# A rolled loop for TensorE's sums, a small first tile and a short second pass in a channel-attention kernel

## The chip, the cores and the metric

The kernel runs on one core of a Trainium2 chip. The time of a run is the device time in microseconds of one launch. Besides, one execution was recorded by the hardware profiler; its span goes from the program's first instruction to its last.

A core has five engines that run side by side, each with its own queue of instructions: TensorE (PE in the profile), VectorE (DVE), ScalarE (ACT), GpSimd (POOL) and SyncE (SP). Sixteen DMA engines move data between the chip's memory and the core's own memory, SBUF. SyncE and ScalarE each own a DMA queue (q1 and q10 in the profile), and a DMA that is issued on either is split evenly over the 16 DMA engines. TensorE writes its results into another memory, PSUM.

## The reference

The input `x` has 384 x 384 pixels of 384 channels in bfloat16, 113 MB, and the output has the same size. Each channel is averaged over all pixels, multiplied by one weight, put through a sigmoid, and the whole channel is multiplied by the result:

```python
g = jnp.einsum("bhwc->bc", x) / (H * W)
...
for i in range(k):
    s = s + gp[:, i:i + C] * w1d[i]
s = _sigmoid(s)
return x * s[:, None, None, :]
```

Here `k` is 1, so there is one weight and no neighbouring channel. The numbers in `x` are normal with a deviation of 0.05, so that every channel's average is almost zero and every scale is close to sigmoid(0) = 0.5.

## The kernel before, in words

A scale depends on all pixels, so a plain kernel would read `x` twice. This one reads it once: it works out an early scale from the first tile of pixels, multiplies every tile by it and stores the result, and meanwhile sums all of `x`. At the end it works out the true scale and compares it, in bfloat16, with the early one. Only where the two differ in any channel does a second pass read `x` again and store the right product. In this data they are the same, and the second pass is skipped by a branch.

**Tiles.** The pixels are cut into 1152 "rows" of 128 x 384 numbers, one pixel for each of SBUF's 128 partitions; a row takes 768 B of each partition. The arena holds 272 rows and is used as six slots of 44 rows. There are 27 tiles (`sizes`, line 165): 25 of 44 rows, one of 28 and one of 24. Tile `k` lies in slot `k % 6`. In `dram` (line 129) each partition gets pixels that are next to each other, so a tile of 44 rows is 128 pieces of 33792 B, eight for each DMA engine.

**Loads.** The first four tiles (`BOTH`, line 115) are loaded in halves, one on SyncE's queue and one on ScalarE's, in packets of 16896 B; the weight follows the first half on ScalarE's queue (line 281). All later tiles are loaded on SyncE's queue alone. From the seventh tile on a load must wait until the store of the tile six back has landed (`Planner.dma`, line 80, works out the waits).

**Sums.** `add_rows` (line 199) multiplies a tile by a matrix of ones, 33 matmuls of 128 x 512 for 44 rows, and lets them add up in three PSUM banks: group 0 for the first tile (its sum gives the early scale), group 1 for all others. The first matmul is line 185, the others are line 187. All 864 are written out one after another in TensorE's program.

**Early scale.** VectorE adds the banks' six parts (`add_banks`, lines 227 and 229), ScalarE takes the sigmoid (line 288).

**Gate and store.** `put` (line 234) multiplies a tile by the early scale on VectorE (line 159), in place, so after TensorE has summed the tile; the store goes out on ScalarE's queue. The last tile alone is written to another slot (line 306), so that its gate needs only its load.

**Order.** `Planner` keeps a stream of operations for each engine and works out which semaphores each must wait for. The streams are emitted in the order in which the Python code adds them: in the loop of line 297, for tile `k`, the gate and store of tile `k - 6`, the load of `k`, the sum of `k`. The first loads go out ahead of everything else (`heads`, line 282).

**End.** After the last tile VectorE adds group 1 to the total, ScalarE takes the sigmoid (line 312), VectorE compares (320), reduces (328) and converts to a flag (334). In `second_pass` (line 362) SyncE, VectorE and ScalarE each load the flag and branch past the second pass, 27 tiles of load, gate and store in their programs. ScalarE then waits for all stores (line 398).

Of the kernel before, what the change touches and what calls it, by code (L numbers as in the profile page):

```python
# [3 lines left out]
P = 128  # L4
ROW = 384
BF16 = mybir.dt.bfloat16
# [7 lines left out]
class Planner:  # L14
# [9 lines left out]
    def __init__(self, nc, name, n_dma_sems):  # L24
        self.nc = nc
        self.streams = {e: [] for e in ("sync", "scalar", "vector", "tensor", "gpsimd")}
        self.sems = {e: nc.alloc_semaphore(f"{name}_{e}") for e in self.COMPUTE}
        self.count = {e: 0 for e in self.COMPUTE}
        self.pool = [nc.alloc_semaphore(f"{name}_dma_{i}") for i in range(n_dma_sems)]
        self.pool_uses = [0] * n_dma_sems  # L30
        self.n_dma = 0
        self.writer = {}
        self.readers = {}
        self.seen = {e: {} for e in self.streams}
        self.final = []

    def _wait(self, engine, token):
        sem, value = token
        if self.seen[engine].get(sem.name, 0) >= value:
            return  # L40
        self.seen[engine][sem.name] = value
        self.streams[engine].append(("wait", sem, value))

    def _needs(self, reads, writes):
        need = {}
        tokens = []
        for r in reads:
            if r in self.writer:
                tokens.append(self.writer[r])
        for r in writes:  # L50
            if r in self.writer:
                tokens.append(self.writer[r])
            tokens.extend(self.readers.get(r, ()))
        for sem, value in tokens:
            if need.get(sem.name, (None, 0))[1] < value:
                need[sem.name] = (sem, value)
        return list(need.values())

    def _record(self, token, reads, writes):
        for r in reads:  # L60
# [5 lines left out]
    def op(self, engine, emit, reads=(), writes=(), signal=True):  # L66


        reads, writes = list(reads), list(writes)
        for token in self._needs(reads, writes):  # L70
            if engine == "tensor" and token[0].name == self.sems["tensor"].name:
                continue
            self._wait(engine, token)
        token = (self.sems[engine], self.count[engine] + 1)
        if signal:
            self.count[engine] += 1
        self.streams[engine].append(("op", emit, self.sems[engine] if signal else None, 1))
        self._record(token, reads, writes)

    def dma(self, engine, out, in_, reads=(), writes=()):  # L80
        reads, writes = list(reads), list(writes)
        for token in self._needs(reads, writes):
            self._wait(engine, token)
        i = self.n_dma % len(self.pool)
        self.n_dma += 1
        if self.pool_uses[i]:
            self._wait(engine, (self.pool[i], 16 * self.pool_uses[i]))
        self.pool_uses[i] += 1
        token = (self.pool[i], 16 * self.pool_uses[i])
        self.streams[engine].append(  # L90
            ("op", lambda e: e.dma_start(out, in_), self.pool[i], 16)  # L91
        )
        self._record(token, reads, writes)
        return token

    def emit(self, name, e, most=None):

        now = self.streams[name][:most]
        del self.streams[name][: len(now)]
        for kind, a, b, *c in now:  # L100
            if kind == "wait":
                e.wait_ge(a, b)
            else:
                ins = a(e)
                if b is not None:
                    ins.then_inc(b, c[0])
# [5 lines left out]


WIDE = 512
EDGE, SLOT, BOTH = 44, 44, 4


def bass_standalone__channel_attn_eca__vision_kernel(
# [12 lines left out]

    ones = nc.alloc_sbuf_tensor("ones", [P, P], BF16)
    s_early = nc.alloc_sbuf_tensor("s_early", [P, C], BF16)
    s_true = nc.alloc_sbuf_tensor("s_true", [P, C], BF16)
    w_one = nc.alloc_sbuf_tensor("w_one", [1, 16], BF16)
    w_scaled = nc.alloc_sbuf_tensor("w_scaled", [P, 2], F32)
    warm = nc.alloc_sbuf_tensor("warm", [P, 2], F32)
    wrong = nc.alloc_sbuf_tensor("wrong", [P, 1], F32)
    redo = nc.alloc_sbuf_tensor("redo", [P, 1], I32)
# [18 lines left out]
        v, to_v = (at(r, n).rearrange("p (t c) -> p t c", t=n) for r in (place, to))  # L158
        return lambda e: e.tensor_tensor(to_v, v, s_b, ALU.mult)  # L159

    n_slots = n_arena // SLOT
    full, rest = divmod(n_rows - EDGE, SLOT)
    if rest < EDGE:
        full, rest = full - 1, rest + SLOT
    sizes = [EDGE] + [SLOT] * full + [4 * q for q in split(rest // 4, EDGE // 4)]
    assert sum(sizes) == n_rows and max(sizes) <= SLOT
    plan = Planner(nc, "a", 50)

    def load(place, n, r0, queues=("sync",)):
        of = dram(x_rows, r0, n)  # L170
        i = 0
        for queue, m in zip(queues, split(n, -(-n // len(queues)))):
            plan.dma(
                queue,
                at(place + i, m),
                of[:, i * C : (i + m) * C],
                writes=rows(place + i, m),
            )
            i += m
# [16 lines left out]
            )  # L196
        )

    def add_rows(place, n, group, first, last):

        n_wide = n * C // WIDE
        start = place * C
        for i in range(n_wide):
            bank = acc[group][i % 3]
            plan.op(
                "tensor",
                lambda e, i=i, bank=bank: mm(e,
                    bank[:, :],
                    ones[:],
                    arena[:, start + i * WIDE : start + (i + 1) * WIDE],  # L210
                    start=first and i < 3,
                    stop=last and i >= n_wide - 3,
                ),
                reads=["ones"] + (rows(place, n) if i in (0, n_wide - 1) else []),
                writes=[f"acc{group}"],
                signal=i == n_wide - 1,
            )

    def add_banks(group, copy):

# [10 lines left out]
                )  # L231
            plan.op("vector", emit, reads=[f"acc{group}", "total"], writes=["total"])

    def put(place, n, r0, to):
        plan.op(
            "vector",
            gate(to, place, n, s_early),
            reads=["s_early"] + rows(place, n),
            writes=rows(to, n),
        )  # L240
        plan.final.append(
            plan.dma("scalar", dram(o_rows, r0, n), at(to, n), reads=rows(to, n))
        )

    def weight():
# [12 lines left out]
            reads=["ones", "w_one"],  # L258
            writes=["w_all"],
        )  # L260
        for i, n in enumerate((sizes[0], n_rows)):
            plan.op(
                "vector",
                lambda e, i=i, n=n: e.tensor_scalar_mul(  # L264
# [3 lines left out]
                writes=[f"w_scaled{i}"],  # L268
            )

    starts = [sum(sizes[:k]) for k in range(len(sizes))]
    places = [k % n_slots * SLOT for k in range(len(sizes))]
    last = len(sizes) - 1


    plan.op("gpsimd", lambda e: e.memset(warm[:, 0:1], 0.0), writes=["warm"])  # L276
    plan.op("vector", lambda e: e.memset(ones[:], 1.0), writes=["ones"])  # L277
    for k in range(BOTH):
        load(places[k], sizes[k], starts[k], ("sync", "scalar"))
        if k == 0:  # L280
            plan.dma("scalar", w_one[0:1, 0:1], w1d.unsqueeze(0), writes=["w_one"])
    heads = {e: len(plan.streams[e]) for e in ("sync", "scalar")}
    weight()
    add_rows(places[0], sizes[0], 0, True, True)
    add_banks(0, copy=True)
    plan.op(
        "scalar",
# [3 lines left out]
        reads=["total", "w_scaled0", "warm1"],  # L291
        writes=["s_early"],
    )

    for k in range(1, len(sizes)):
        if k >= n_slots:
            j = k - n_slots
            put(places[j], sizes[j], starts[j], places[j])  # L300
        if k >= BOTH:
            load(places[k], sizes[k], starts[k])
        add_rows(places[k], sizes[k], 1, k == 1, k == last)
    for k in range(len(sizes) - n_slots, last):
        put(places[k], sizes[k], starts[k], places[k])
    put(places[last], sizes[last], starts[last], places[last + 1 - n_slots])


    add_banks(1, copy=False)
    plan.op(  # L310
        "scalar",
        lambda e: e.activation(  # L312
            s_true[:], total[:], ACT_F.Sigmoid, scale=w_scaled[:, 1:2]
        ),
        reads=["total", "w_scaled1"],
        writes=["s_true"],
    )
    plan.op(
        "vector",
        lambda e: e.tensor_tensor(  # L320
            total[:], s_true[:].bitcast(U16), s_early[:].bitcast(U16), ALU.not_equal
        ),
        reads=["s_true", "s_early"],
        writes=["total"],
# [13 lines left out]
    checked = (plan.sems["vector"], plan.count["vector"])  # L338


    again = Planner(nc, "b", 50)
    for place, n, r0 in zip(places, sizes, starts):
        again.dma("sync", at(place, n), dram(x_rows, r0, n), writes=rows(place, n))
        again.op(
            "vector",
            gate(place, place, n, s_true),
            reads=rows(place, n),
            writes=rows(place, n),
        )
        again.final.append(  # L350
            again.dma("scalar", dram(o_rows, r0, n), at(place, n), reads=rows(place, n))
        )
    for token in again.final:
        again._wait("scalar", token)
    stored = nc.alloc_semaphore("stored")
# [71 lines left out]
```

## Time and profile before

| what | us |
|---|---|
| median of 8 runs | 529.92 (529.63 to 530.01) |
| the profiled execution | 530.15 |
| its span, first to last instruction | 528.69 |
| TensorE busy, of that | 242.5 |
| VectorE busy | 241.2 |
| ScalarE busy | 2.7 |
| last load has landed, last gate starts | 496.45 |
| last store is issued | 501.4 |
| flag of the second pass is ready | 507.2 |

| DMA | |
|---|---|
| bytes moved | 226.57 MB |
| mean rate over the span | 429 GB/s |
| a load on SyncE's queue, 44 rows, issue to landing | 38.4 us |
| a store, 44 rows, issue to landing | 62.4 us |

The page lists busy time by engine, then the span in 40 slices, then the DMA queues with their packets, megabytes and share of the 16 engines' time. The queues q8 and q14, called "instruction", carry the engines' own programs from the chip's memory. In a line of the timeline the columns are start, length, engine, line, operation, and in brackets how long the engine sat idle before it and what ended that. A busy TensorE is not TensorE at its peak, and idle time of an engine that is not the bottleneck costs nothing. The trace also holds each DMA packet's start, length, queue and size.

### The profile page before, as it was taken

The page shows a single profiled execution, that of the slowest core. Times are in us where ns is not written, and L with a number is a line of the kernel's source. Part 1 is how long each engine was busy: PE and PEld are TensorE (multiplying, and loading weights), DVE is VectorE, ACT ScalarE, POOL GpSimd, SP SyncE. Part 2 cuts the span into 40 slices and gives each one's busy share as a digit, 9 for nine tenths or more (in the row PEclk, how much of TensorE's full clock was granted, in tenths as well). Part 3 has the DMA queues.
Part 4 walks back from the last instruction along what each step waited for, and adds up shares of the span by engine and source line. Part 5 has one row for each costly group of instructions (what it writes and reads, how often), then busy time and mean ns, then how long its engine had stood idle before and what let it go on. Part 6 is the DMA issues. An engine that isn't in the chain of part 4 may idle for free.

```text
span 528.7 us, 1091 instructions
## 1 busy us (share of the span) xinstructions
PE 242.5 (46%) x865; PEld 0.2 (0%) x2; DVE 241.2 (46%) x45; ACT 2.7 (1%) x4; POOL 0.3 (0%) x5
## 2 busy tenths in 40 slices
PE   0876356065165274274164274374363363375400
PEld 0000000000000000000000000000000000000000
DVE  0199741632633624624624624615624615616720
ACT  1000000000000000000000000000000000000000
POOL 0000000000000000000000000000000000000000
PEclk9998786686786786776786886775786876876765
DMA  8999999999999999999999999999999999999998
GB/s 358 431 426 422 447 412 446 435 427 442 417 447 424 437 442 417 447 421 440 435 424 445 422 442 435 424 445 417 445 433 424 442 419 445 426 444 419 446 421 351
DMA packets 8360, 226.57 MB, mean 429 GB/s; under 512 B 930, under 2 KB 930, under 8 KB 930
## 3 DMA queue, kind: packets, MB, share of 16 engines
q10 hardware_dynamic: 4466, 121.90, 53.5%
q1 hardware_dynamic: 3888, 104.60, 46.1%
q8 instruction: 3, 0.05, 0.0%
q14 instruction: 3, 0.02, 0.0%
HBM read 113.25 MB, written 113.25 MB: 428 GB/s over the span
## 4 chain that ended last, share of the span: by engine, by line
another core or an unknown queue 70%; DMA 16%; DVE 4%; PE 3%; SPq 1%; issue 1%; ACT 0%; ACTq 0%
DMA out_dram<-arena 8%; DMA arena<-in_x_dram 6%; PE acc L187 3%; DVE arena L159 3%; DMA w_one<-in_w1d_dram 2%; SPq L91 1%; DVE total L229 1%; ACT s_early L288 0%; ACT s_true L312 0%; DVE total L227 0%; DVE total L320 0%; DVE wrong L328 0%; PE acc L185 0%; ACTq L91 0%
## 5 line engine op out<-in xcount | busy, mean ns | idle before, releaser
L187 PE MATMUL acc<-arena,ones 128*128 128x512 bf16 x863 | 242.0, 450 | 245.7 <-DMA arena<-in_x_dram 245.7
L159 DVE TENSOR_TENSOR arena<-arena,s_early 128x16896 bf16<-128x16896 bf16 (+2 forms) x27 | 234.5, 8692 | 240.2 <-PE acc L187 237.4
L255 PE MATMUL w_all<-w_one,ones 1*128 1x1 bf16 x1 | 0.2, 158 | 14.3 <-DMA w_one<-in_w1d_dram 14.3
L264 DVE TENSOR_SCALAR w_scaled<-w_all 128x1 f32<-128x1 f32 x2 | 0.2, 154 | 13.5 <-PE w_all L255 13.5
L229 DVE TENSOR_TENSOR total<-total,acc 128x128 f32<-128x128 f32 (+2 forms) x11 | 4.5, 409 | 1.4 <-PE acc L187 1.1
L227 DVE COPY total<-acc 128x384 f32<-128x384 f32 x1 | 0.6, 558 | 9.3 <-PE acc L187 9.3
L312 ACT ACTIVATE s_true<-total,w_scaled 128x384 bf16<-128x384 f32 x1 | 0.6, 616 | 477.8 <-DVE total L229 477.8
L249 ACT ACT_TABLE_LOAD x1 | 1.3, 1283 | 3.4 <-issue 3.4
L320 DVE TENSOR_TENSOR total<-s_true,s_early 128x384 f32<-128x384 uint16 x1 | 0.6, 558 | 0.7 <-ACT s_true L312 0.7
L288 ACT ACTIVATE s_early<-total,w_scaled 128x384 bf16<-128x384 f32 x1 | 0.6, 617 | 21.9 <-DVE total L229 21.9
L185 PE MATMUL acc<-arena,ones 128*128 128x512 bf16 x1 | 0.6, 586 | 0.0
L328 DVE TENSOR_REDUCE wrong<-total 128x1 f32<-128x384 f32 x1 | 0.6, 553 | 0.0
L277 DVE MEMSET ones<- 128x128 bf16 x1 | 0.2, 165 | 0.8 <-PEq L412 0.8
L249 ACT ACTIVATE warm<-warm 128x1 f32<-128x1 f32 x1 | 0.2, 203 | 0.0
L334 DVE CAST redo<-wrong 128x1 int32<-128x1 f32 x1 | 0.2, 153 | 0.0
L255 PEld LDWEIGHTS w_all<-w_one,ones 1*128 1x128 bf16 x1 | 0.1, 101 | 14.2 <-issue 14.2
L185 PEld LDWEIGHTS acc<-arena,ones 128*128 128x128 bf16 x1 | 0.1, 102 | 0.0
L412 POOL MEMSET const-bfloat16-1.0<- 128x1 bf16 x1 | 0.1, 102 | 0.0
L412 POOL MEMSET const-uint8-127<- 128x1 uint8 x1 | 0.1, 102 | 0.0
L276 POOL MEMSET warm<- 128x1 f32 x1 | 0.1, 99 | 0.3 <-POOLq L412 0.3
L412 POOL MEMSET const-float32-0.0<- 128x1 f32 x1 | 0.1, 99 | 0.2 <-issue 0.2
L412 POOL MEMSET const-float32-1.0<- 128x1 f32 x1 | 0.1, 99 | 0.0
## 6 DMA issues: line engine op xcount, KB each, us to landing
out_dram<-arena ACTq DMA_DIRECT2D x25, 4224.0 KB, 62.4
arena<-in_x_dram SPq DMA_DIRECT2D x21, 4224.0 KB, 38.4
arena<-in_x_dram ACTq DMA_DIRECT2D x4, 2112.0 KB, 27.4
arena<-in_x_dram SPq DMA_DIRECT2D x4, 2112.0 KB, 27.0
arena<-in_x_dram SPq DMA_DIRECT2D x1, 2688.0 KB, 35.0
out_dram<-arena ACTq DMA_DIRECT2D x1, 2688.0 KB, 28.7
arena<-in_x_dram SPq DMA_DIRECT2D x1, 2304.0 KB
out_dram<-arena ACTq DMA_DIRECT2D x1, 2304.0 KB, 27.2
```

The costliest lines, as they stand in the source:

```text
L91: ("op", lambda e: e.dma_start(out, in_), self.pool[i], 16)
L159: return lambda e: e.tensor_tensor(to_v, v, s_b, ALU.mult)
L185: loaded.append(e.matmul(bank, weights, moving, start=start, stop=stop))
L187: return e.add_instruction(mybir.InstMatmult(name=nc.get_next_instruction_name(), engine=mybir.EngineType.PE, ins=[e.lower_ap(moving), e.l ...
L227: emit = lambda e, part=part, of=of: e.tensor_copy(part, of)
L229: emit = lambda e, part=part, of=of: e.tensor_tensor(part, part, of, ALU.add)
L249: lambda e: e.activation(warm[:, 1:2], warm[:, 0:1], ACT_F.Sigmoid),
L288: lambda e: e.activation(s_early[:], total[:], ACT_F.Sigmoid, scale=w_scaled[:, 0:1]),
L312: lambda e: e.activation(s_true[:], total[:], ACT_F.Sigmoid, scale=w_scaled[:, 1:2]),
L320: lambda e: e.tensor_tensor(total[:], s_true[:].bitcast(U16), s_early[:].bitcast(U16), ALU.not_equal),
L328: lambda e: e.reduce_max(wrong[:], total[:], axis=mybir.AxisListType.X),
L412: nc = _bacc.Bacc("TRN2", target_bir_lowering=False, num_devices=1)
```

## The change

Nothing of what is computed changes. The parts:

- **Sizes.** The first tile has 8 rows, loaded in halves of 4 on both queues; the early scale comes from the first 4 rows alone (`EARLY`). The other 1144 rows are 26 tiles of 44. The 8 rows have a place of their own behind the six slots, stay there to the end, and are gated and stored last. The tiles in halves on both queues are the four that follow, and the loads of the other two slots go out ahead as well.
- **TensorE's program.** The matmuls of the six slots are written once, as the body of a loop of five rounds; in the last round a branch leaves out four of the six slots. Three matmuls on zeros close the sum. Since a loop can't wait for a different semaphore in each round, GpSimd waits for each load and then counts up one semaphore, `ready`; TensorE waits for it ahead of each slot and counts it down.
- **Last tile.** It is gated in place, after its sum.
- **Waits.** `Planner` now knows what each semaphore's value implies and leaves out waits that another wait covers.
- **Second pass.** Nine pieces of 128 rows in two halves of the arena take the place of the 27 tiles.
- **True scale.** It has no tensor of its own but lies in the arena, in the slot of tile 20.

```diff
-EDGE, SLOT, BOTH = 44, 44, 4
+FIRST, EARLY, TILE, SLOTS, BOTH = 8, 4, 44, 6, 4
...
+        return [
+            (sem, value)
+            for sem, value in need.values()
+            if not any(
+                self.clocks[s.name, v].get(sem.name, 0) >= value
+                for s, v in need.values()
+                if s.name != sem.name
+            )
+        ]
...
+    def relay(self, sem, via, to, first, reads, writes):
+
+        if first:
+            self.need(via, first)
+            self.streams[via].append(("op", lambda e: e.sem_inc(sem, 1), None, 0))
+            for name, at in self.seen[via].items():
+                self.seen[to][name] = max(self.seen[to].get(name, 0), at)
+        self.signals(to, reads, writes)
...
+    def sum_others():
+
+        none = zeros[:, 0:1].broadcast_to([P, WIDE])
+
+        def one(e, s):
+            e.wait_ge(ready, 1).then_inc(ready, -1)
+            add_rows(e, 1, slot(s) * C, TILE, False, False).then_inc(
+                plan.sems["tensor"], 1
+            )
+
+        def emit(e):
+            add_rows(e, 1, (base + EARLY) * C, FIRST - EARLY, True, False)
+            rounds = -(-n_tiles // SLOTS)
+            some = n_tiles - (rounds - 1) * SLOTS
+            with e.Fori(0, rounds) as k:
+                for s in range(some):
+                    one(e, s)
+                if some < SLOTS:
+                    with e.If(k < rounds - 1):
+                        for s in range(some, SLOTS):
+                            one(e, s)
+            for i in range(3):
+                out = mm(e, acc[1][i][:, :], ones[:], none, False, True)
+            out.then_inc(plan.sems["tensor"], 1)
...
+    load(base, FIRST, 0, ("sync", "scalar"))
+    plan.dma("scalar", w_one[0:1, 0:1], w1d.unsqueeze(0), writes=["w_one"])
     for k in range(BOTH):
-        load(places[k], sizes[k], starts[k], ("sync", "scalar"))
...
+        load(slot(k), TILE, row0(k), ("sync", "scalar"))
+    for k in range(BOTH, SLOTS):
+        load(slot(k), TILE, row0(k))
...
+    for k in range(n_tiles):
+        if k >= SLOTS:
+            put(slot(k), TILE, row0(k - SLOTS))
+            load(slot(k), TILE, row0(k))
+        there = rows(slot(k), TILE)
+        plan.relay(ready, "gpsimd", "tensor", there, there, ["acc1"])
+    plan.signals("tensor", rows(base, FIRST), ["acc1"])
+    for k in range(n_tiles - SLOTS, n_tiles):
+        put(slot(k), TILE, row0(k))
+    put(base, FIRST, 0)
...
-    again = Planner(nc, "b", 50)
-    for place, n, r0 in zip(places, sizes, starts):
+    again = Planner(nc, "b", 30)
+    half, r0 = base // 2, 0
+    s_kept = at(base, 1)
...
+    for k, n in enumerate(split(n_rows, half)):
+        place = k % 2 * half
```

## The prediction

> **What bounds the kernel now.** I read the page first: busy engines, the slices, the queues.
>
> ```profile
> span 528.7 us, 1091 instructions
> ...
> PE 242.5 (46%) x865; PEld 0.2 (0%) x2; DVE 241.2 (46%) x45; ACT 2.7 (1%) x4; POOL 0.3 (0%) x5
> ...
> DMA  8999999999999999999999999999999999999998
> ...
> q10 hardware_dynamic: 4466, 121.90, 53.5%
> q1 hardware_dynamic: 3888, 104.60, 46.1%
> q8 instruction: 3, 0.05, 0.0%
> q14 instruction: 3, 0.02, 0.0%
> ```
>
> TensorE and VectorE work under half the time; the DMA engines work throughout. Then the table of stretches: the steady middle, and both ends (columns: length, busy time by engine, clock, DMA share, GB/s).
>
> ```profile
> 60.00:460.00 400.00, 186.18 (x660) 0.00 (x0) 180.56 (x21) 0.00 (x0) 0.00 (x0) 0.73 1.00 433
> ...
> 526.00:528.70 2.70, 0.00 (x0) 0.00 (x0) 0.00 (x0) 0.00 (x0) 0.00 (x0) 0.50 0.18 75
> 0.00:2.50 2.50, 0.00 (x0) 0.00 (x0) 0.17 (x1) 0.00 (x0) 0.30 (x5) 1.00 0.48 108
> ```
>
> In the middle the share is 1.00 at 433 GB/s. All 226.57 MB at that rate take 523.3 us, so 5.4 us of the span are lost at its ends: at the start 2.5 us move 0.27 MB (worth 0.6), 1.9 lost; at the end 2.7 us move 0.20 MB (worth 0.5), 2.2 lost; the rest (1.3) is smaller packets and the turn from loads to stores near 44 us. Bytes stay the same, so only these 5.4 us can be won.
>
> The end I followed in the trace's DMA packet records, where each engine's next packet starts within a few ns of the last one's end. Ten of the 16 engines end between 526.0 and 526.5, six at 526.72, 527.02, 527.59, 527.65, 527.78 and 528.17; the last instruction ends 0.52 after the last of them. Every engine has the same 464 data packets, so the late ones did something besides. Three met a q8 packet (16384 B of instructions; at 89.6, 229.4 and 389.2 us). Each stood 0.94 us, its next packet took 0.37 longer: 1.31 us, never caught up, and the three account for 527.59 to 527.78. The queue part of a 2-us window shows one.
>
> ```profile
> q10 hardware_dynamic: 16, 0.54, 63.7%
> q1 hardware_dynamic: 12, 0.41, 46.9%
> q8 instruction: 1, 0.02, 3.0%
> ```
>
> 3.0% of 16 engines for 2 us is 0.96 us of one engine. The last engine, 528.17, has no q8 packet: from about 140 to 488 us its packets run some 3.5 ns longer (1.0 us in all), and a q14 packet at 512.0 costs it 0.57. The other q14 packets (492.4, 513.0) cost 0.8 and 0.4 on other engines.
>
> **The change part by part.**
>
> *The loop.* TensorE's 865 matmuls become a body of 6 x (33 + 1 wait) = 204 instructions, about 20 around it, run five times (the last round two slots). What it does to TensorE is hidden: it waits some 10.5 us per tile for loads (464.71 in the last fence). What reaches the end is the fetches. The first came while tile 6 was summed, the third in tile 21: 15 tiles of 33, up to a tile more, so 248 to 264 instructions per 16384 B. Counted from the code, tile 6 starts near TensorE's instruction 209; even spacing puts the first trigger at 209 to 217. The new body runs from about 16 to 224: it crosses this point once per round and then jumps back. [...] I take one to five, on different engines as the three were; both ends stay in the range.
>
> [...]
>
> *What goes, and what is late next.* With one to three fetches on separate engines the late engines stay at 526.2 + 1.31 plus 0.1 to 0.3 of phase, 527.5 to 527.8. The slow engine is late by 1.0 + 0.1 without any fetch: 527.3, and 528.1 if a q14 packet meets it again. So the end moves from 528.17 to 527.3 at best and 528.2 at worst; I take 527.7, a gain of 0.5.
>
> *Shorter second pass, fewer waits.* It is skipped (its flag is zero), so it costs nothing in time before and after; what is left is where the branch past it lands. Two q14 packets come 5 to 6 us after the check ends at 507.2, so I take them for the branch's. With 9 pieces instead of 27 the jump is shorter by some 20 to 35 instructions per queue. Bounds: all three q14 packets stay (0), or go (0.4 to 0.8 on three engines, only the slow one matters: 0.57). I count half in the 0.5 above.
>
> *The small first tile.* 3072 B packets in, 6144 out. A 16896 B packet takes 629 ns, 33792 B 1251, so a packet costs 7 ns beyond its bytes; 8 packets more per engine are 0.06 us. Bounds: 0.06, and 0.5 if short packets at the cold start stall as the turn at 44 us does (406 against 433 GB/s over 40 to 48: 0.5). I take 0.15, nearest to the packet rows. The early scale is ready near 5 us instead of 27.4, but the first store cannot use it: tile 0 must land (about 16), be summed (9.2) and gated (9.0), and the scalar queue holds loads to about 44 us (92 rows at half rate), as it did to 42.5. Worth 0: that queue was never empty.
>
> *Relay through GpSimd.* Each tile: a GpSimd wait, an increment, a wait on TensorE. Nothing else is queued on GpSimd; behind TensorE's wait stand only that tile's matmuls. The trace does not show it: from 0 to 1.0 us per tile (the chain of waits has 0.33 for SyncE's step from a landed store to the next load; three such steps), under 10.5 us of idle time. The three closing matmuls on zeros add 0.9 at the end. Free.
>
> *The last tile.* Its gate now waits for its sum, where the old one wrote to another slot at once. The old end:
>
> ```profile
> 464.71 9.73 PE L187 MATMUL acc<-arena,ones 128*128 128x512 bf16 x33 [10.49 <-DMA arena<-in_x_dram]
> ...
> 481.03 7.51 PE L187 MATMUL acc<-arena,ones 128*128 128x512 bf16 x21 [6.59 <-DMA arena<-in_x_dram]
> 488.65 5.76 DVE L159 TENSOR_TENSOR arena<-arena,s_early 128x10752 bf16<-128x10752 bf16 x1 [5.14 <-PE acc L187]
> 496.45 4.96 DVE L159 TENSOR_TENSOR arena<-arena,s_early 128x9216 bf16<-128x9216 bf16 x1 [2.04 <-DMA arena<-in_x_dram]
> 496.46 5.98 PE L187 MATMUL acc<-arena,ones 128*128 128x512 bf16 x18 [7.92 <-DMA arena<-in_x_dram]
> ```
>
> Line 187 takes 9.73 for 44 rows (first row), line 159 takes 8.96 (group by form). A load lands 38.4 us after issue, issued when the store six tiles back landed; stores advance one tile per 19.95, so 1.92 tiles meanwhile, and 6 - 1.92 = 4.1 tiles wait to be stored. A tile is 4.325 MB, 10.0 us: behind the last load stand 41 us plus 1.8 for the 8 rows. The last tile's store is issued 9.7 + 9.0 = 18.7 us after landing; 31 us of other stores cover it, 12 us to spare. Behind that gate queue the 8 rows' gate (1.6), six adds (2.7), the sigmoid and the check (2.5): ready some 27 us after landing, under 42.6. The true scale now goes into tile 20's slot and so waits for that tile's store, which has landed by then: only the last 4.1 tiles are out. If the cover is gone (TensorE stalled by over 12 us in the last rounds) each us more is lost. Free.
>
> Sum against the profiled execution (530.15; 1.46 outside its span, left as it is): 530.15 - 0.5 + 0.15 = 529.8; the median of the runs is 0.23 lower, so 529.55.
>
> **Rivals.**
>
> *A, forecast: an even trade,* 529.55. Fetches fewer or differently spread, yet another engine ends last. For it: the last engine today has no TensorE fetch. Its own range: 528.9 to 530.6 (the end at 527.3 to 528.2, small packets to 0.5).
>
> *B, the end closes up: faster.* No TensorE fetch, and the slow engine's drift or its q14 packet gone too: all end by 526.5. 528.17 - 526.5 = 1.7, less 0.15: 528.4. For it: the code barely exceeds one block; short code can remove both kinds of fetch. Against it: the drift has no source that the change removes.
>
> *C, the jump refetches: slower.* Place: the back edge. Price: 1.31 us per fetch, all on the DMA engine that carries it. Nine spread evenly cost nothing beyond today's; the time decides from three on one engine, or two on the slow one: 526.2 + 3 x 1.31 + 0.2 = 530.3, 2.2 later: 532.0; two on the slow one, 526.2 + 1.1 + 2.6 = 529.9: 531.6. Four on one: 533.4. For it: the trigger lies inside the body. Against: three fetches of before fell on three engines.
>
> *D, the change does not do what it says:* as many fetches as now, on other engines. The time is A's, near 529.9. I count it there.
>
> **How the numbers follow.** A with D 0.45, B 0.2, C 0.3, and 0.05 for a lost cover or a slow start, slower by 1 to 2 us. The bound of 0.2% is 1.06 us, about what a measurement of this kernel can tell from no change: faster below 528.86, slower above 530.98. So faster 0.2, same 0.45, slower 0.35. Range: down to B's 528.4, up to C's 532.0, which leaves out about 2 in 10. No case has much over half; A's own range is given above.
>
> **What would show it.** The count of q8 packets: one (A, B), nine or so (C), three (D). The stretch 526 to the end: 0.5 us shorter under A; several us at a tenth of the rate under C. The last gate must follow TensorE's sum at least 10 us before the store queue runs dry; the middle must stay at 433 GB/s. If the middle's rate moves, or the DMA share at the start falls below 0.48, my account of where time can change is wrong.

## The result, and the profile after

The changed kernel takes 535.51 us (median of 11 runs, 531.44 to 541.34); the kernel before took 529.89 beside it (31 runs, 529.63 to 530.20). The ratio is 1.0076, 95% interval 1.0057 to 1.0095, so it is slower by more than 0.2%, and the median lies 3.5 us above the range that was predicted. The ratio leaves out runs that lie over 1.5% above a kernel's own fastest; here the scatter of the runs is part of the effect, and the medians alone stand at 1.0106. The profiled execution took 535.38 us, with a span of 533.8.

The page of the changed kernel: its span, the DMA engines by slice, and the queues.

```profile
span 533.8 us, 1112 instructions
...
DMA  8999999999999999999999999999999999999995
GB/s 359 428 430 414 438 428 430 433 425 430 430 430 436 433 428 436 433 428 441 433 420 436 436 420 441 433 420 438 430 413 441 428 428 443 428 425 433 437 430 250
...
q10 hardware_dynamic: 4610, 122.29, 53.2%
q1 hardware_dynamic: 3888, 104.20, 45.8%
q8 instruction: 1, 0.02, 0.0%
q14 instruction: 2, 0.02, 0.0%
```

The bytes are the same (226.53 MB), one 16384 B fetch is left of three, and the DMA engines are still busy throughout. What differs is the last slice, 5 tenths instead of 8, and small dents in the rate. The table of stretches has the same in numbers (length, busy time by engine, clock, DMA share, GB/s):

```profile
60.00:460.00 400.00, 192.19 (x660) 0.00 (x0) 179.06 (x21) 0.00 (x0) 0.00 (x0) 0.71 1.00 431
526.00:533.00 7.00, 0.00 (x0) 0.00 (x0) 0.00 (x0) 0.00 (x0) 0.00 (x0) 0.50 0.36 154
```

Between 60 and 460 us the DMA share is 1.00 as before, but it moves 431 GB/s, not 433. 2 in 433 of 400 us is 1.8 us on the mean of 16 engines; and they do not lose it alike, for from 526 to 533 us only 0.36 of them still work. In the packet records nearly every full load packet (33792 B) after 60 us took 1251 ns in the kernel before (2555 of 2575), none over 1272. In the changed kernel 143 of 2698 took 50 to 976 ns longer (I call these long load packets), 2.0 us on the mean engine and over 5 us on three of them. So a load's 16 shares land ever further apart: within 2.2 us in the first tiles, within 8.6 in the last. Thirteen engines end between 526.5 and 529.5 us, three at 533.3 to 533.4.

The end of the timeline (start, length, engine, line, operation, and in brackets the idle time and what ended it):

```profile
490.91 8.73 PE L238 MATMUL acc<-arena,ones 128*128 128x512 bf16 x33 [11.82 <-PEq L279]
499.48 0.81 PE L238 MATMUL acc<-zeros,ones 128*128 128x512 bf16 x3
499.68 10.63 DVE L202 TENSOR_TENSOR arena<-arena,s_early 128x16896 bf16<-128x16896 bf16 x2 [11.59 <-PE acc L238]
...
514.77 0.15 DVE L414 CAST redo<-wrong 128x1 int32<-128x1 f32 x1
```

TensorE waits 11.82 us ahead of its last tile, and it waited ahead of the tiles before (26 waits, 248.3 us in all): the loop stands on no path that sets the end. The check is ready at 514.9, the last stores run to 533.4.

### The profile page after: what moved, and what is told of

Its sections match the earlier page's. It is cut to its first block, busy times and chain, and to the rows that moved or that the text cites. A ratio compares the mean times of both kernels' runs of the same rounds, so it can differ in the third digit from the quotient of the medians.

```text
span 533.8 us, 1112 instructions
## 1 busy us (share of the span) xinstructions
PE 246.8 (46%) x868; PEld 0.2 (0%) x2; DVE 241.1 (45%) x45; ACT 2.7 (1%) x4; POOL 0.3 (0%) x6
## 2 busy tenths in 40 slices
DMA packets 8501, 226.53 MB, mean 424 GB/s; under 512 B 946, under 2 KB 946, under 8 KB 1330
## 5 line engine op out<-in xcount | busy, mean ns | idle before, releaser
L238 PE MATMUL acc<-arena,ones 128*128 128x512 bf16 x863 | 245.6, 455 | 248.3 <-PEq L279 248.3
L202 DVE TENSOR_TENSOR arena<-arena,s_early 128x16896 bf16<-128x16896 bf16 (+1 forms) x27 | 234.5, 8691 | 266.3 <-PE acc L238 266.3
L236 PE MATMUL acc<-arena,ones 128*128 128x512 bf16 x1 | 0.6, 606 | 0.3 <-DMA arena<-in_x_dram 0.3
```

Of the source, the lines that this page charges most:

```text
L236: loaded.append(e.matmul(bank, weights, moving, start=start, stop=stop))
L238: return e.add_instruction(mybir.InstMatmult(name=nc.get_next_instruction_name(), engine=mybir.EngineType.PE, ins=[e.lower_ap(moving), e.l ...
```

## The experiments

The expectations number the theories as they came up. Where they end: the loop, the address of the tiles and the short packets themselves cost nothing that can be measured (529.81 us for all of the change with the weight's DMA on another queue, 530.04 for the kernel before with its tiles moved); ScalarE's queue runs dry for 1.6 us near 5 us because the weight's DMA stands ahead of the first half, this gives SyncE's queue a lead (2.1 turns at 13 us) that lasts, and a lead of one packet on most engines does harm by itself (539.50 us in the kernel before; theories 7 and 8). With leads that differ from engine to engine runs are slow too (four of 12 at 535.2 to 537.7 us with steps of 3 to 5), in a way that stays open.

A word for what follows. In the packet records each DMA engine alternates between the two queues, packet by packet: from 60 to 460 us 5734 of 5746 packets in the kernel before, and 5672 of 5730 in the changed one, follow a packet of the other queue. A tile's share on one engine is 8 packets and a landing packet (4 B, 9 ns), nine turns. I call **step** the number of load packets on an engine between the landing of a load and the next landing of a store. In the kernel before it is 0 on 15 engines and 2 on the one that carried the weight's packet and its landing packet. The step was read by chaining the packets of an engine, the start of one to the end of the last; where two engines' packets end at the same instant the chains can be exchanged.

### The loop, the addresses, the first tile

**The 8 rows taken from the end of `x`,** so that the other tiles start where they did before:

```diff
-        return FIRST + k * TILE
+        return k * TILE
-    load(base, FIRST, 0, ("sync", "scalar"))
+    load(base, FIRST, n_rows - FIRST, ("sync", "scalar"))
...
```

> The changed kernel, but its small tile is the last 8 rows of x instead of the first 8, so that each large tile starts at a multiple of 44 rows again, as before the change. In the changed kernel some load packets take 0.05 to 0.9 us longer than 1.251, at moments that come every 20 us, and the loads' landings spread over the 16 DMA engines by 2.2 us at first and 8.6 at the end. Theory 1 (addresses: the shift by 8 rows makes loads and stores meet in memory): the long packets go, the spread stays under 4 us, 529.3 to 530.3 us. Theory 2 (short packets at the start put the engines out of step, and that grows): no change, 531 to 541. Theory 3 (TensorE's loop or the relay): no change, 531 to 541.

Measured: 533.91 (529.71 to 541.18, 10 runs), ratio 1.0026 (0.9995 to 1.0058). The runs fall in two heaps, 529.7 to 531.0 and 536.9 to 541.2, and the profiled one (539.61) has 400 long load packets. Half the runs are as slow as before this edit, although the large tiles start where they did in the old kernel: the address alone is not it.

**The loop written out,** 26 tiles' matmuls one after another in the changed kernel:

```diff
-            with e.Fori(0, rounds) as k:
...
+            for k in range(n_tiles):
+                one(e, k % SLOTS)
```

> The changed kernel with the 26 tiles' matmuls written out one after another, with the same waits on the relayed semaphore; all else as changed. Theory 3 (the loop costs the time): back to 529.5 to 530.3, with three q8 packets. Theories 1 and 2 (addresses, start): 531 to 541 as changed, about 0.3 us more or less for the two extra q8 packets, with the same spread of landings.

Measured: 537.26 (533.02 to 540.82, 4 runs), ratio 1.0111 (1.0050 to 1.0172), three fetches, 174 long load packets. Without a loop it is as slow; the loop is not it.

**The kernel before with all tiles moved by 8 rows:**

```diff
-    sizes = [EDGE] + [SLOT] * full + [4 * q for q in split(rest // 4, EDGE // 4)]
+    sizes = [EDGE] + [SLOT] * full + [28, 16, 8]
...
-    starts = [sum(sizes[:k]) for k in range(len(sizes))]
+    starts = [(8 + sum(sizes[:k])) % n_rows for k in range(len(sizes))]
```

> The kernel before with every tile moved by 8 rows in x and in the output (tiles of 44 rows from row 8 on, then 28, 16, and 8 rows from row 0 as the last); TensorE written out, no short packets at the start. Theory 1: slower, 531 to 541, long load packets in the middle. Theories 2 and 3: 529.5 to 530.5, steady packets of 1.251 us.

Measured: 530.04 (529.95 to 531.06), ratio 1.0005 (0.9996 to 1.0015), no long packet. The address falls from this side too.

**The 8 rows as one DMA on SyncE's queue,** in packets of 6144 B; ScalarE's queue so starts with the weight:

```diff
-    load(base, FIRST, 0, ("sync", "scalar"))
+    load(base, FIRST, 0)
```

> The changed kernel, but the small tile's 8 rows come in one DMA on SyncE's queue in packets of 6144 B, not in two halves of 3072 B on both queues. Theory 2: fewer engines out of step at the start, so the spread of landings starts nearer to 0.4 and the time falls, 529.5 to 533. Theories 1 and 3: 531 to 541, unchanged spread.

Measured: 540.52 (539.36 to 571.63, 4 runs), ratio 1.0197 (1.0173 to 1.0222), the highest median of all; what made one run take 571.63 is not known. Its engines leave the start within 0.9 us of each other and drift apart only later, so a start made ragged by short packets is not it. What it shares with the slow ones is the weight ahead of the first half on ScalarE's queue.

### The weight's DMA

**Behind the first half again,** where the kernel before has it, nothing else undone:

```diff
     load(base, FIRST, 0, ("sync", "scalar"))
-    plan.dma("scalar", w_one[0:1, 0:1], w1d.unsqueeze(0), writes=["w_one"])
     for k in range(BOTH):
         load(slot(k), TILE, row0(k), ("sync", "scalar"))
+        if k == 0:
+            plan.dma("scalar", w_one[0:1, 0:1], w1d.unsqueeze(0), writes=["w_one"])
```

> The changed kernel with one DMA moved: the weight's is issued on ScalarE's queue behind the first half of the first large tile, not ahead of it. New theory 4 (step of the queues): before, ScalarE's queue never ran dry at the start and on every DMA engine the two queues' tiles begin and end together; in the changed kernel it holds only 4 rows when the weight's DMA is issued (0.54 us), runs dry, and SyncE's queue is 3 us ahead from then on, so that the tiles of loads and stores turn at different moments, and near these turns load packets take up to 0.9 us longer. It expects the landings on the two queues together again (within 1 us in the first 45 us), no long packets after 50 us, a spread under 4 us, and 528.8 to 530.0 us. Theory 2 (short packets at the start): unchanged, 531 to 541.

Measured: 530.01 (529.38 to 530.68, 11 runs), ratio 0.9999 (0.9990 to 1.0008), no long load packet. One DMA of two bytes, one place later in its queue, gives back the whole loss. In the table of stretches the middle is at 433 again:

```profile
60.00:460.00 400.00, 187.36 (x646) 0.00 (x0) 180.80 (x21) 0.00 (x0) 0.00 (x0) 0.72 1.00 433
526.00:533.00 7.00, 0.00 (x0) 0.00 (x0) 0.00 (x0) 0.00 (x0) 0.00 (x0) 0.71 0.07 31
```

**The same, with the matmuls written out,** so that the loop can be priced without the disturbance:

> The same with TensorE's matmuls written out. Theory 4: 529.3 to 530.4, and by the difference to the looped one what the loop is worth once nothing else disturbs: the prediction's 0.5 us or less for one fetch in place of three. Theories 2 and 3: 531 to 541.

Measured: 530.21 (529.39 to 530.65, 11 runs), ratio 1.0001 (0.9992 to 1.0010). Three fetches against one, 0.2 us apart: too little to tell from none.

### Is it the number of packets in each queue?

Theory 4 said that a queue which is some packets behind the other costs time. The kernel before got spare packets: DMAs into an unused tensor, one packet on each engine for 16 partitions, and a landing packet.

```diff
+    spare = nc.alloc_sbuf_tensor("spare", [P, C], BF16)
...
+            plan.dma("scalar", spare[0:64, :], x_rows[0:64, :], writes=["spare"])
```

**First tile split 26 to 18 rows** in place of 22 to 22 (packets of other sizes, the same number):

> The kernel before with the first tile split 26 rows on SyncE's queue and 18 on ScalarE's instead of 22 and 22; nothing else. Theory 4: the two queues are out of step by 8 rows from the first tile on, load packets become longer near the turns and the spread of landings grows: 531 to 545 us. Theories 2 and 3 (short packets, loop): no change, 529.7 to 530.5.

Measured: 529.92 (529.83 to 530.29), ratio 1.0000 (0.9991 to 1.0009); step 0 as before. The engines took turns by packets here too, with 19968 B in one queue's and 13824 B in the other's.

**Four spare packets on ScalarE's queue:**

> The kernel before and one more DMA on ScalarE's queue behind the weight's: 64 partitions of 768 B into a spare tensor that nothing reads, so 4 packets more per DMA engine on that queue; nothing else. The step is the number of data packets per engine that the load queue has done more than the other, modulo 8 (a tile is 8 packets per engine and queue): 1 in the kernel before and in every fast run so far, 2 to 3 in the slow ones. The uneven split left it at 1, since the engines take packets of the two queues in turn whatever their size. Theory 4 in this form (out of step by packets, nothing else): step 5 here, long load packets, spread growing, 531 to 541. Theory 2 (it takes the short packets at the very start): 529.8 to 530.3.

**Eight:**

> The same with 128 partitions: 8 packets more per DMA engine, a whole tile's count, so that the step is 1 again modulo 8. Theory 4: 529.8 to 530.5, no long packets in the middle. A theory that any extra DMA at the start disturbs the engines: as slow as with 4 packets.

**Four on SyncE's queue:**

> The 4 extra packets per engine on SyncE's queue instead, step 1 - 4 modulo 8, again 5, from the other side. Theory 4: 531 to 541 as with the other queue. A theory in which only a late store queue costs time: 529.8 to 530.3.

**Two on ScalarE's:**

> The kernel before with the spare DMA of 32 partitions, 2 packets more per DMA engine on ScalarE's queue. Read engine by engine, the step (load packets that an engine does between the end of a load tile and the end of the next store tile on the other queue) is 0 on 15 engines in the kernel before and its fast variants; 5 and 4 with four packets more on the one or the other queue, and these ran at 530.4 and 530.3 without long packets, so that being out of step is not what costs. In the slow kernels it is 1, 2 or 3. Theory 4 narrowed (a step of 1 to 3 costs): 533 to 541, long load packets just behind the load's turn, spread growing. Theory 5 (the step is a bystander; something else that the small tile brings, such as its place or the early start of stores, makes the load packets long): 529.8 to 530.5.

**One on ScalarE's:**

> The same with 16 partitions, one packet more per DMA engine: a step of 1. Theory 4 narrowed: 533 to 541 as in the variant that has a step of 1 on nearly all engines (540.5). Theory 5: 529.8 to 530.5.

| spare packets per engine | step, on most engines | us | ratio |
|---|---|---|---|
| 4 on ScalarE's queue | 5 | 530.38 | 1.0009 (0.9999 to 1.0019) |
| 8 on ScalarE's | 9, later 4 and 5 | 531.49 | 1.0031 (1.0018 to 1.0043) |
| 4 on SyncE's | 4 (nine less five) | 530.31 | 1.0008 (0.9998 to 1.0017) |
| 2 on ScalarE's | 3 | 530.15 | 1.0005 (0.9995 to 1.0014) |
| 1 on ScalarE's | 2 | 530.24 | 1.0005 (0.9995 to 1.0014) |

With eight, the loss of 0.3% is clear of noise: there is one burst of long packets, which ends at 90 us, and none after it. Steps of 2 to 5 cost 0.1% at most by these ratios, so theory 4 fell. The row with step 1 is missing: n spare packets and their landing packet make a step of n + 1.

### A dry queue, or one engine out of line?

In every kernel that kept its time so far, one DMA engine carried the weight's packet among full packets and so stood two turns out of line; in every slow one the weight came earlier. Theory 6 took this for a protection, theory 7 took the early weight for the harm.

**The changed kernel with the weight on GpSimd's queue:**

```diff
-    plan.dma("scalar", w_one[0:1, 0:1], w1d.unsqueeze(0), writes=["w_one"])
+    plan.dma("gpsimd", w_one[0:1, 0:1], w1d.unsqueeze(0), writes=["w_one"])
```

> The changed kernel, with only the weight's one-element DMA moved from ScalarE's queue to GpSimd's. ScalarE's queue so holds its 4-row piece and then the large halves, with no small DMA between, but also no DMA engine that is one packet out of line with the others. Theory 6 (the one-element packet, when it stands between full packets of ScalarE's queue, puts one DMA engine out of line, and this engine's early and late landings keep the others together; in the changed kernel it comes too early for that): still slow, 531 to 541 us, no engine that lands its share of every load some 1.9 us ahead. Theory 7 (the weight's issue between the 4-row piece and the first half lets ScalarE's queue run dry at the start, and the engines leave the start in groups): 529.4 to 530.7, landings of a load within 4 us on all engines. The old prediction's account (the order of the weight is worth nothing, the loss is the small tile): 531 to 541.

Measured: 529.81 (529.40 to 530.92, 11 runs), ratio 0.9997 (0.9988 to 1.0006); no engine out of line, all within 1.2 us to the end. Theory 6 falls. ScalarE's queue at the start of the timeline, changed kernel first, then this one (ACTq is the issue of a DMA):

```profile
0.73 0.41 ACTq L109 DMA_DIRECT2D arena<-in_x_dram  x1
1.18 0.54 ACTq L109 DMA_DIRECT2D w_one<-in_w1d_dram  x1
1.75 2.42 ACTq L109 DMA_DIRECT2D arena<-in_x_dram  x4
```

```profile
0.74 2.92 ACTq L109 DMA_DIRECT2D arena<-in_x_dram  x5
```

And what the two queues moved between 4.2 and 5.8 us (packets, MB, share of the 16 engines), in the same order:

```profile
q1 hardware_dynamic: 41, 0.56, 86.3%
q10 hardware_dynamic: 14, 0.03, 5.3%
```

```profile
q10 hardware_dynamic: 27, 0.29, 44.8%
q1 hardware_dynamic: 24, 0.30, 44.1%
```

Here is the dry queue. In the changed kernel the weight takes 0.54 us to issue, the first half is issued at 1.75 and its first packet starts at 6.25 us (median of the engines), while the four rows ahead of it have landed at 4.03: 2.2 us without a data packet, and SyncE's queue has the engines alone. With the weight elsewhere the half starts at 4.68, 0.65 after the four rows: one packet of the other queue (629 ns). So the queue is dry for 1.6 us.

**The changed kernel with a second one-element DMA behind the first half:** the start as dry as it was, but one engine out of line.

```diff
         load(slot(k), TILE, row0(k), ("sync", "scalar"))
+        if k == 0:
+            plan.final.append(
+                plan.dma("scalar", w_one[0:1, 8:9], w1d.unsqueeze(0), writes=["w_two"])
+            )
```

> The changed kernel, its early weight DMA kept where it is, and a second one-element DMA added on ScalarE's queue behind the first half of the first large tile (into an unused element, so nothing that is computed changes). The start is as dry as in the changed kernel, but one DMA engine is one packet out of line from some 14 us on. Theory 6 (the out-of-line engine protects): 529.4 to 530.7, as when the weight itself stood there. Theory 7 (the dry start does the harm): 531 to 541, landings of a load spread over 6 to 9 us at the end.

Measured: 540.07 (531.65 to 541.39, 6 runs), ratio 1.0202 (1.0188 to 1.0216). Theory 7 holds. Its profiled execution is by chance its quickest (531.65), and shows the harm at its beginning: all of its 31 long load packets lie on five engines, and on each of them only while its step is 1 (on one until 92 us, on another until 128, on a third from 148 us on); the eleven with steps of 2, 3 and 5 have none.

**The kernel before with the weight on GpSimd's queue:**

```diff
-    plan = Planner(nc, "a", 50)
+    plan = Planner(nc, "a", 70)
...
-            plan.dma("scalar", w_one[0:1, 0:1], w1d.unsqueeze(0), writes=["w_one"])
+            plan.dma("gpsimd", w_one[0:1, 0:1], w1d.unsqueeze(0), writes=["w_one"])
```

> The kernel before, with only the weight's one-element DMA moved to GpSimd's queue (and 70 semaphores for DMAs in place of 50, so that GpSimd's has its own). No packet stands between the halves on ScalarE's queue, so no DMA engine is out of line; the first tile stays as it was, both queues full from the start. Theory 6: slower, 531 to 541 us, with long load packets in the middle. Theory 7: as before, 529.6 to 530.4, since no queue ran dry at the start.

Measured: 529.95 (529.73 to 530.20, 11 runs), ratio 1.0000 (0.9991 to 1.0009). Nothing to protect.

How a gap of 1.6 us lasts 530 us is seen in the landings of the first large tile's two halves (medians of the 16 engines). Two packets, one of each queue, take 1.258 us.

| kernel | SyncE's half lands | ScalarE's half | lead in turns | steps |
|---|---|---|---|---|
| before | 12.58 | 12.59 | 0.0 | 0 |
| changed, weight behind the half | 14.39 | 14.39 | 0.0 | 0 |
| changed, weight on GpSimd | 14.23 | 14.23 | 0.0 | 0 |
| changed, 8 rows in one DMA | 13.75 | 15.00 | 1.0 | 1 |
| changed, 8 rows from the end | 13.54 | 15.46 | 1.5 | 1 and 2 |
| changed | 13.06 | 15.68 | 2.1 | 1, 2 and 3 |
| changed, second element | 12.52 | 16.08 | 2.8 | 1 to 5, mostly 3 |

The lead of the start is the step of the middle, and in the changed kernel nothing takes it back: at 50, 100, 200 and 400 us three engines stand at step 1, seven at 2 and six at 3. The three at step 1 are the three that end last (533.3 to 533.4 us), and carry about half of the time that its long packets cost.

### A step of one packet

**The kernel before with a step of 1,** made of two spare DMAs: two packets on ScalarE's queue, one on SyncE's (3 - 2 = 1).

```diff
...
+            plan.dma("scalar", spare[0:32, :], x_rows[0:32, :], writes=["spare"])
+            plan.dma("sync", spare2[0:16, :], x_rows[0:16, :], writes=["spare2"])
```

> The kernel before, with two spare DMAs behind the first tile's halves: 32 partitions of one row on ScalarE's queue (two packets and a landing packet for each DMA engine) and 16 partitions on SyncE's (one packet and a landing packet). Each alone moved nothing (530.15 and, on ScalarE's queue, 530.24 us); together they put the store's landing one packet of the load stream behind the load's landing on 15 engines, the step that the engines with the most long load packets have in the changed kernel (step 1: 5.0 to 5.4 us of long packets; step 2: 0.4 to 2.3; step 3: 0.8 to 3.0). Nothing runs dry. Theory 8 (a step of one packet between a load's landing and a store's landing on the same DMA engine makes its load packets long): 533 to 541 us, long load packets on 15 engines. Theory 7 in its narrow form (a queue that runs dry at the start sorts the engines into groups, and only the spread among engines does the harm): 529.9 to 530.7, as with each spare DMA alone.

Measured: 539.50 (537.40 to 541.43, 5 runs), ratio 1.0186 (1.0164 to 1.0209), 313 long load packets, on all 16 engines. The middle of its table of stretches:

```profile
60.00:460.00 400.00, 180.09 (x647) 0.00 (x0) 175.96 (x20) 0.00 (x0) 0.00 (x0) 0.74 1.00 426
526.00:533.00 7.00, 0.00 (x0) 0.00 (x0) 0.00 (x0) 0.00 (x0) 0.00 (x0) 0.50 0.86 370
```

426 GB/s, in the old kernel, with no dry queue, no loop and no small tile. One of the 16 engines, the one that carries the weight's packets too, stands at step 3 throughout and still has 6.2 us of long packets, about as much as the others. So the harm isn't confined to an engine's own step: what the run shows is a step of 1 on 15 engines slowing all 16.

**Its mirror image,** the sizes exchanged (2 - 3 = -1, a step of 8):

```diff
...
+            plan.dma("scalar", spare[0:16, :], x_rows[0:16, :], writes=["spare"])
+            plan.dma("sync", spare2[0:32, :], x_rows[0:32, :], writes=["spare2"])
```

> As the run with step 1, but with the sizes exchanged: 16 partitions on ScalarE's queue, 32 on SyncE's, so that the load's landing comes one packet behind the store's (step 8 of 9 instead of 1). The same bytes and DMAs. Theory 8, if it is the nearness of the two landings that counts: 533 to 541 us; if the order of the two counts: 529.9 to 530.7. Theory 7, narrow form: 529.9 to 530.7.

Measured: 530.35 (530.16 to 531.25, 11 runs), ratio 1.0010 (1.0001 to 1.0018), step 8 on most engines, 11 long packets. The same bytes and the same two DMAs cost 0.4 us. So it is not the nearness of the two landings but their order: the store's one packet behind the load's. The weight's engine stands at step 1 here, alone among engines at step 8, and the long packets of all engines together are 1.4 us: one engine at step 1 does little harm.

**The changed kernel with one spare packet on ScalarE's queue,** which turns steps of 1, 2 and 3 into 3, 4 and 5:

```diff
...
+            plan.final.append(
+                plan.dma("scalar", spare[0:16, :], x_rows[0:16, :], writes=["spare"])
+            )
```

> The changed kernel, its dry start and its weight DMA kept, with a spare DMA of 16 partitions of one row on ScalarE's queue behind the first half of the first large tile: one packet and a landing packet more on every DMA engine, so the engines' steps of 1, 2 and 3 become 3, 4 and 5, and the groups stay as far apart from each other as they were. Theory 8 (steps of 1 do the harm): 529.8 to 531 us, no sustained long load packets. Theory 7, narrow form (the spread among the engines does the harm, whatever the step): 531 to 541 us.

Measured: 530.76 (529.59 to 537.69, 12 runs), ratio 1.0033 (1.0005 to 1.0061). The median goes back by 4.8 of 5.6 us, so by the median the steps of 1 are the greater part. But four runs of 12 took 535.2 to 537.7, and the profiled one is of these: 86 long load packets, on engines with steps of 3 and 5, two with step 3 at 5.8 us each while others with step 3 have none. A dry start so has a second way to do harm, which a step of 1 does not explain; engines that differ among each other are common to it and to the changed kernel. The run with the 8 rows from the end shows the same: five of its engines stand at step 2 throughout and have 3.6 to 8.1 us of long packets each, while step 2 on nearly all engines (one spare packet on ScalarE's queue) left one long packet in the whole kernel.

## Why the prediction was wrong

**The step that failed** is the one on the small first tile: "the scalar queue holds loads to about 44 us (92 rows at half rate), as it did to 42.5. Worth 0: that queue was never empty." It was empty for 1.6 us near 5 us. The weight's DMA used to stand behind a half of 22 rows, which kept ScalarE's queue busy to 12.6 us; the diff put it behind a piece of 4 rows, which was through at 4.03. I priced the packets of the small tile (0.06 to 0.5) and left the DMA that was moved along with it out of the sum, though its row, 0.54 us on ScalarE's queue, was in the timeline of before:

```profile
1.17 0.54 ACTq L91 DMA_DIRECT2D w_one<-in_w1d_dram  x1
```

Moving it back or away gives 530.01 and 529.81.

**A second gap in the same step:** even with the dry time on the list I would have written 1.6 us or less, paid once at the start. It cost 5.6 in the median, since the lead it gives one queue decides how two streams meet for the next 480 us. The text named the sign that would show this ("if the middle's rate moves ... my account of where time can change is wrong"); it moved from 433 to 431. Its other sign, a DMA share at the start below 0.48, came as well (0.24 over the first 2.5 us), but it tells nothing: with the weight behind the half it is 0.26, with the weight on GpSimd's queue 0.23, and neither loses time. What I had called "a slow start, slower by 1 to 2 us" got 0.05 and the wrong price.

**The loop** got the count of the lower end, one fetch, as for rivals A and B, but by luck. I had the body cross the place that triggers a fetch in every round, so that the one fetch had to come in the first. It comes at 494.7 us, while the last tile is summed and the loop ends; between 10 and 490 us there is no q8 packet. The queue part of the window from 494 to 496 us:

```profile
q8 instruction: 1, 0.02, 2.9%
```

Written out, with the start repaired, the program fetches first at 151.9 us, while its ninth large tile is summed; the body holds six. So the trigger wasn't inside the body, and C's condition was not met: that the kernel became slower, as C said, has nothing to do with the back edge. C's nine fetches, and the three on one engine behind its 532.0, were a supposition of mine; no run shows a fetch that comes with the jump back. Five looped kernels (the changed one, with the 8 rows from the end, with them in one DMA, with the weight behind the half and with it on GpSimd's queue) had one each. The gain of 0.5 was mis-sized: three fetches against one, with the start repaired, are 530.21 against 530.01, each within 0.1% of before.

**The relay, the last tile and the second pass** are free, as predicted: with the weight elsewhere the whole change stands at 0.9997 (0.9988 to 1.0006). With the weight behind the half, the last large store was issued at 503.66, and the store ahead of it landed from 514.2 on: 10.5 us to spare where 12 were expected. In the changed kernel it was 508.67 against 514.7, 6.0.

**The small tile** itself cost nothing that can be measured (0.15 taken). The early scale was ready at 10.2 us, not near 5, and nothing waited for it. So rival A, the even trade at 529.55, is what the change does without its moved DMA: 529.81.

**Open** stays what makes a load packet take up to 2.2 us in place of 1.25 when stores land one packet behind loads on most engines, why engines at another step are slowed along with them, and why some runs with steps of 3 to 5 suffer too. No run separated the chip's memory from SBUF, or the addresses that the two streams touch at one time. Why the first half's first packet came 4.5 us after its issue behind the weight and 3.5 without it is open as well; the issue of the weight explains 0.54 of the 1.6 us. No version beat the kernel before: the best, 529.81, is the same by its interval.

## What to carry to other kernels

Where two queues share the DMA engines and both stay full, their order at the start can last, as it did here (a lead of 2.1 turns at 13 us, steps of 1 to 3 still at 400): follow each queue's first packets, and count a DMA that is moved there even if it has two bytes. Look whether the bytes ahead of a small DMA last until the next large one moves (here they did not: a piece was through at 4.03 us, the next large one started at 6.25). When a rate that nothing should touch drops by half a per cent (433 to 431 GB/s here), look at single packets before looking at engines: here both the cure and the disease were a packet or two per engine.

## What the runs showed of the hardware

- The engines alternated between the queues by packets (5734 of 5746 in the kernel before), and a landing packet took a turn like any other: 1, 2, 4 spare packets made steps of 2, 3 and 5, and a split of 26 to 18 rows changed none.
- A step of 1 on 15 of the 16 engines costs 1.9% (539.50 against 529.96), its mirror image 0.1%.
- Where leads are mixed, one and the same kernel takes 529.7 in one run and 541.2 in the next; all kernels with a uniform step of 0, 2, 3, 4, 5 or 8 keep their runs within 1.6 us of each other.
- The loop of about 230 TensorE instructions, five rounds, had one 16384 B fetch, at 494.7 us as it ended; written out, three.
